# Three groups of M a batch, scores of batch 2 in fixed banks, and an earlier second weight block

## The chip, the cores and the metric

The kernel runs on one core of a Trainium2 chip. The metric is the time of one execution on the device in microseconds (us), as the median of three runs.

The core has five engines, each with its own in-order queue of instructions: TensorE (PE, matrix products), VectorE (DVE), ScalarE (ACT), GpSimd (POOL) and SyncE (SP, which here issues nearly all DMAs). They wait for one another through semaphores. PE writes to PSUM, which has eight banks of 128 partitions by 512 fp32 numbers. Everything else lives in SBUF or in HBM.

## The reference

Two blocks, one after the other. The first is an attention between 8 batches of 512 rows (8 heads of 64) and 32 states per head; the second is a two-layer network (FFN1, ELU, FFN2) over its output.

```python
scale = 1.0 / np.sqrt(D)                        # B, H, S, Ns, D = 8, 8, 512, 32, 64
a  = softmax(scale * x @ state.T)               # 512 x 32 per head
xread = a @ state
a2 = softmax(scale * state @ x.T)               # 32 x 512 per head
sread = a2 @ x
t = concatenate([xread, sread], axis=2)         # 544 rows per batch, 512 columns
h = t @ w_in                                    # 512 -> 2048
g = where(h > 0, h, exp(minimum(h, 0)) - 1)
out = g @ w_out                                 # 2048 -> 512
```

## The kernel before

**Folding the state into the weights.** `xread @ w_in` is `a @ (state @ w_in)`. So for each batch the kernel makes a matrix M = state @ w_in (256 rows, one for each head and state, by 2048 columns), and FFN1 is then a product of M with aT, the transposed attention weights. M is made from eight blocks of `w_in` of 256 columns each, called `hc` = 0 to 7. `make_m` (line 674) issues 8 matmuls per block on tiles of 64 rows by 32 columns of the array, four blocks of columns side by side. `copy_m` (692) takes the result from two banks to SBUF through ACT. Two neighbouring blocks form a chunk `c` of 512 columns, and FFN1 takes chunks 0 to 3 in turn.

**Fast products.** FFN1 and FFN2 of most batches use Strassen's scheme with seven products instead of eight, so sums of blocks of the operands are needed first: `sum_m` (707) and `sum_a` (716) make those of M and of aT on POOL, `Second.sums` and `combine` (965, 927) those of FFN2's operands on DVE. FFN2 of batches 1 to 7 nests the scheme: each of five outer products is a `Second` (941) with seven products of four matmuls 128x128, and the results are added from PSUM to the output by DVE (or copied by ACT). A product's bank, x or y, is written again by the next product but one.

**Phases.** `start` (1150) handles batches 0 and 1 together while the weights come in: x and state are loaded and transposed, scores and softmax run, blocks of `w_in` are converted to the number format that the products use (`convert`, 1090: two passes on ACT, four or five on DVE), each block is kept in a DRAM copy `w_in_mem`, and then `w_out` is converted too. `w_step(hc)` (1184) converts a block, makes its M for batches 0 and 1 and copies it out. FFN2 of batch 0 follows, then `ffn2_1` (1364) for batch 1, then `batch(b)` (1434) for b = 2 to 7, and `states` (1519) for the rows of `sread`.

**What batch b makes for b + 1.** In `ffn2` (1285) of batch b, `first_m` (1275) makes the M blocks 0 and 1 of batch b + 1, and `scores` makes its scores, in banks 6 and 7, which are called `fixed`. `soft_next` (1329) then runs the softmax in two forms: `softmax` for aT (subtraction of the maximum and the product with the reciprocal of the sum on POOL, transposes and maxima and sums on DVE, exponentials on ACT), and `softmax_rows` for `sread`. `move_state` (797) rearranges the latter with 16 small DMAs on SP, `state_read` (810) uses it. Later in `ffn2` blocks 2 and 3 of M are made; in `batch(b + 1)` 4 and 5, then 6 and 7. Each block comes from `w_in_mem` by `fetch` (669) into one of three slots, `w_half[:, hc % 3]`.

**What sets the order.** The code first records every operation in a `Plan` (87) with an estimated cost, and then a list scheduler (`run`, 239) decides in which order each engine's instructions are issued. PE takes the first operation in the order of recording that could start; DVE, ACT and SP take the one with the earliest due time, worked out backwards from PE's order; POOL keeps the recorded order strictly. A bank is given to an operation when it is free, except that the fixed ones wait for bank 6 or 7. The resulting queues are fixed in the program. In the first 40 us the scheduler also puts in filler matmuls on an identity (line 1590) where it expects PE to have nothing to do. `ident_ready` (1137) puts four matmuls of 128x128 into each fixed bank, before FFN2 of batch 1; nothing reads them.

Of the kernel before, what the change touches and what calls it, by code (L numbers as in the profile page):

```python
# [86 lines left out]
class Plan:  # L87
# [108 lines left out]
    def prepare(self):  # L196
        for op in self.ops:
            op.users = []
            op.turn = self.places.get(op.number, op.number)
        for op in self.ops:  # L200
            for d in op.deps:
                d.users.append(op)
        self.opening = {}
        self.closing = {}
        for b in self.banks:
            self.opening.setdefault(b.first, []).append(b)
            self.closing.setdefault(b.last, []).append(b)
        self.kept = {b.first: b.fixed for b in self.fixed}
        self.all_banks = min([op.number for op in self.kept], default=0)
# [29 lines left out]
    def run(self, until=0.0):  # L239
# [8 lines left out]
        banks = [(0.0, i) for i in range(self.BANKS)]  # L248
        fixed = set(self.kept.values())
        openers = sorted((op for op in self.ops if op in self.opening), key=lambda op: op.turn)  # L250
# [8 lines left out]
        def bank_time(op):  # L259

            if op in self.kept:
                return min([t for t, i in banks if i == self.kept[op]], default=None)
            need = len(self.opening[op])
            if op is not openers[oldest] and op.number > self.all_banks:
                need += self.KEPT_BANKS
            free = choice(op)
            return free[need - 1][0] if need <= len(free) else None
# [40 lines left out]
        while len(done) < len(self.ops):  # L308
# [26 lines left out]
            if op in self.kept:  # L335
                banks = [b for b in banks if b[1] != self.kept[op]]
                if self.kept[op] in holder:
                    after.append((holder[self.kept[op]], op))
            while oldest < len(openers) and openers[oldest] in opened:
# [50 lines left out]
def kernel(  # L390
# [165 lines left out]
    def bank():  # L556
        return Bank(plan).view()
# [116 lines left out]
    def make_m(b, *hcs):  # L674
# [11 lines left out]
        if hcs[-1] % 2 == 0:  # L686
            plan.ops[-1].spare = st[b, "m", c][0].bank

    def m_blocks(m):
        return [m[:, g * 512 + h * 256 : g * 512 + (h + 1) * 256] for h in range(2) for g in range(2)]  # L690
# [25 lines left out]
    def sum_a():  # L716

        r11, r12, r21, r22 = a_blocks_of(a_sb)
        t1, t2, t4 = (a_sb[:, 1024 + 256 * i : 1280 + 256 * i] for i in range(3))
        (V if 0 else Q).tensor_tensor(out=t1, in0=r12, in1=r11, op=ALU.subtract)  # L720
        (V if 0 else Q).tensor_tensor(out=t2, in0=r22, in1=t1, op=ALU.subtract)
        (V if 0 else Q).tensor_tensor(out=r12, in0=r22, in1=r12, op=ALU.subtract)
        (V if 0 else Q).tensor_tensor(out=t4, in0=r21, in1=t2, op=ALU.subtract)

# [35 lines left out]
    def softmax(b, to):  # L760
        s = st[b, "s"]
        total_t = small(b)[:, 36:68]

        def rows(g):
            return soft_t(b, g).rearrange("p (k n) -> p k n", n=NS)

        for g in range(G):
            V.transpose(out=soft_t(b, g), in_=s[g])
        for g in range(G):
            V.reduce_max(out=tops(b, g)["top_t"], in_=rows(g), axis=AX_X)  # L770
            (V if 0 & 1 and b > 1 or b in [] else Q).tensor_tensor(
                out=rows(g), in0=rows(g), in1=bc(tops(b, g)["top_t"], NS), op=ALU.subtract
            )
            A.activation(out=soft_t(b, g), in_=soft_t(b, g), func=AF.Exp, scale=scale)
            V.reduce_sum(out=tops(b, g)["total_t"], in_=rows(g), axis=AX_X)
        line(b, total_t, 1.0, eps)
        V.reciprocal(out=total_t, in_=total_t)
        for g in range(G):
            (V if 0 & 2 and b > 1 or b in [] else Q).tensor_tensor(
                out=rows(g), in0=rows(g), in1=bc(tops(b, g)["total_t"], NS), op=ALU.mult  # L780
            )
            V.transpose(out=to[:, g * 512 : (g + 1) * 512], in_=soft_t(b, g))
# [158 lines left out]
    class Second:  # L941
# [39 lines left out]
        def steps(self, out, fresh=False, base=None):  # L981

            t, s = self.t_w, self.s
            a11, a12, a22 = self.a
            x, y = bank(), bank()
            steps = []

            def step(n, ps, a, b, first, last, h, c):
# [9 lines left out]
                    "second",  # L998
                )
                o, p = (x[:, h, c * P : (c + 1) * P] for x in (out, base or out))  # L1000
                if n not in (0, 2, 3, 6):
                    p = o
                elif fresh:
                    p = None
# [6 lines left out]

            for n, args in enumerate((
                (x, a11, self.b11, True, False, 0, 0),
                (y, a12, self.b21, True, True, 0, 0),
                (x, s[2], t[2], False, False, 1, 0),
                (y, s[3], t[3], True, False, 1, 1),
                (x, s[1], t[1], False, False, 1, 1),
                (y, a22, t[4], False, True, 1, 0),
                (x, s[4], self.b22, False, True, 0, 1),
            )):  # L1020
                steps.append(lambda n=n, args=args: step(n, *args))
            return steps
# [127 lines left out]
    def start():  # L1150
# [21 lines left out]
        n = len(plan.ops)  # L1172
        load_states(0, 1, raw_s, (SP, ACT))
        load_x(0, x_halves, (SP, ACT))
        blocks[0] = weight_block(0, 2)
        load_states(1, 2, raw_s[:, 1:], (SP,))
        load_x(1, x_1)
        read_block(1)
        read_block(2)
        for k, op in enumerate(plan.ops[n:]):  # L1180
# [3 lines left out]
        def w_step(hc):  # L1184
            convert_block(hc)
            w = st["w", hc] = w_half[:, hc % 3]
# [14 lines left out]

        turn_x(x_halves, ob, 1)
        scores(0, ob)
        softmax(0, a_sb)
        w_step(0)
        ffn1(0, 0, (0, 1), 0 & 1)
        turn_x(x_1, ob)
        scores(1, ob)
        softmax(1, aT1)
        ffn1(1, 0, (0, 1), 0 & 2)  # L1210
        w_step(1)
        ffn1(0, 0, (2, 3))
        ffn1(1, 0, (2, 3))
        for c in range(1, 4):
            w_step(2 * c)
            w_step(2 * c + 1)
            ffn1(0, c)
            if c < 2:
                for b in range(2):
                    softmax_rows(b)  # L1220
                    turn_state(b)
                    state_read(b, (x_halves, x_1)[b])
            ffn1(1, c)
# [35 lines left out]
        o.copy(y, 1, 1)  # L1259
        scores(2, xr)  # L1260
        softmax(2, a_sb)
# [13 lines left out]
    def first_m(b, at=None):  # L1275
# [6 lines left out]
        fetch(2)  # L1282
        fetch(3)

    def ffn2(o, b):
# [3 lines left out]
        spare = spaces(m_sb[:, 1], 3)  # L1289
        o.sum_1()  # L1290
        late = [plan.ops[-1]]
        if 0:
            second[1].sums(o.a11, spare + s_2[0][:1])
            steps = second[1].steps(c12, fresh=True)
            steps[0]()
        else:
# [3 lines left out]
            steps = []  # L1300
        if nxt:
            first_m(b + 1, 1)
            scores(b + 1, xr, [f.view() for f in fixed])
        else:
            turn_read()
        for f in steps[1:]:
            f()
        second[2].sums(o.a12, s_2[1] + spaces(a_sb))
        late.append(plan.ops[-1])
        for f in second[2].steps(c11, base=c12):  # L1310
            f()
        late.append(plan.ops[-1])
        second[4].sums(o.a22, s_2[0] + spare[:2])
        late.append(plan.ops[-1])
        for f in second[4].steps(c21, fresh=True):
            f()
        second[6].sums(o.s, s_2[1] + spaces(a_sb))
        late.append(plan.ops[-1])
# [10 lines left out]
        def soft_next():  # L1329
            if nxt:  # L1330
                with plan.behind(late[4]):
                    softmax(b + 1, a_sb)
# [22 lines left out]
        if nxt:  # L1355
            make_m(b + 1, 2, 3)
            copy_m(b + 1, 1, m_to[1])
            sum_m(m_to[1])
            state_read(b + 1)
        for f in steps:  # L1360
# [3 lines left out]
    def ffn2_1(o, b, x1):  # L1364
# [30 lines left out]
        second[3].sums(o.a12, s_2[0])  # L1395
        make_m(b + 1, 2, 3)
        copy_m(b + 1, 1, m_to[1])
        sum_m(m_to[1])
        state_read(b + 1)
        for f in steps:  # L1400
# [33 lines left out]
    def batch(b):  # L1434
        for hc in range(4, 7):
            fetch(hc)
# [6 lines left out]
        p[0][0]()  # L1443
        p[1] = ffn1_chunk(b, 1, g_sb)
        p[0][1]()
        make_m(b, 4, 5)
        fetch(7)
        copy_m(b, 2, m_to[2])
        sum_m(m_to[2])
        p[1][0]()  # L1450
        p[2] = ffn1_chunk(b, 2, g_sb)
        p[1][1]()
        make_m(b, 6, 7)
        copy_m(b, 3, m_to[3])
        sum_m(m_to[3])
        if b + 1 < B:
# [122 lines left out]
    o, x1 = start()  # L1579
    ident_ready(0)  # L1580
    ident_ready(1)
    ffn2_1(o, 1, x1)
# [49 lines left out]
```

## Time and profile before

| | |
|---|---|
| median of three runs | 702.73 us (702.24 to 704.44) |
| the profiled execution | 704.65 us |
| its span, first to last instruction | 702.9 us |
| granted TensorE clock, mean | 0.997 |
| PE busy | 692.8 us (99%) |
| DVE busy | 563.8 us (80%) |
| ACT busy | 303.9 us (43%) |
| POOL busy | 144.2 us (21%) |
| DMA | 78.55 MB, mean 112 GB/s |

The span is that of the instructions; the profiled execution's own time is 1.75 us more. Busy shares are averages over the whole span, and the stages differ. These are the page's busy tenths in 40 equal slices of 17.6 us (9 is 90% or more):

```profile
PE   8899999999999999999999999999999999999997
DVE  4899999999649985899669985998589966997650
ACT  4899982011148122742176215712373227500530
POOL 1300000052211062303530181116220453000000
```

The first slices are the start with its loads; from the third on PE is full. DVE has nine tenths from 35 to 175 us, and ACT to 88 us, where weights are converted. From the twelfth slice on a pattern repeats about every 76 us, one batch: FFN1, with more work for ACT, and FFN2, with more for DVE.

Among the groups of instructions, POOL's are

```profile
L464 POOL TENSOR_TENSOR m<-m 128x256 f32<-128x256 f32 x72 | 63.6, 907 | 52.0 <-ACT m L464 50.6
L464 POOL TENSOR_TENSOR aT<-aT 128x256 f32<-128x256 f32 x24 | 22.3, 950 | 1.4 <-DVE aT L464 1.4
```

The columns are line, engine, operation, what it writes and reads, shapes and count, then the sum in us and the mean in ns, then the engine's idle time before. The first are the sums of M, the second those of aT.

### The profile page before, as it was taken

Reading aid. Unit: us, or ns where it says so; the run is one execution under the profiler, and the core shown is the slowest. Engines: PE = TensorE matmul, PEld = TensorE weight load, DVE = VectorE, ACT = ScalarE, POOL = GpSimd, SP = SyncE. Lnnn points to the kernel's source line nnn. Section 1 sums busy time; section 2 is a strip of 40 time slices with the busy share of each in tenths; the row PEclk is TensorE's granted clock in tenths of the full one; section 3 lists DMA queues with packets and bytes.
Section 4 is the critical chain, followed back from the end, with each engine's and each line's share of the span. In section 5 each row is a group of like instructions: output and inputs, shape, how many; then the busy total and the mean of one; then the engine's idle time right before and its main releaser. Section 6 shows DMA issues by size and latency. Waiting matters only on the chain.

```text
span 702.9 us, 14562 instructions
## 1 busy us (share of the span) xinstructions
PE 692.8 (99%) x5794; PEld 591.0 (84%) x5794; DVE 563.8 (80%) x991; ACT 303.9 (43%) x628; POOL 144.2 (21%) x161
## 2 busy tenths in 40 slices
PE   8899999999999999999999999999999999999997
PEld 7544468889988998889988998899888997899996
DVE  4899999999649985899669985998589966997650
ACT  4899982011148122742176215712373227500530
POOL 1300000052211062303530181116220453000000
PEclk9999999999999999999999999999999999999999
DMA  8578774204262505740471417450565034200300
GB/s 213 189 261 274 239 249 73 61 31 120 71 140 92 121 11 152 171 115 8 120 182 56 95 29 194 108 122 14 153 165 121 1 120 152 61 1 31 121 8 23
DMA packets 111268, 78.55 MB, mean 112 GB/s; under 512 B 89184, under 2 KB 92768, under 8 KB 111200
## 3 DMA queue, kind: packets, MB, share of 16 engines
q1 hardware_dynamic: 108988, 77.06, 39.4%
q8 instruction: 46, 0.75, 0.4%
q10 hardware_dynamic: 2212, 0.56, 0.4%
q14 instruction: 22, 0.18, 0.1%
HBM read 61.34 MB, written 13.11 MB: 106 GB/s over the span
## 4 chain that ended last, share of the span: by engine, by line
PE 94%; ACT 2%; DMA 2%; DVE 1%; SPq 1%; issue 0%; ACTq 0%; DVEq 0%
PE ps L464 93%; DMA g<-in_x_dram 1%; DMA xe<-in_x_dram 1%; SPq L464 1%; DVE w_half L464 1%; ACT sec L464 1%; ACT w_half L464 0%; ACT t_w L464 0%; PE ps L1590 0%; ACT m L464 0%; DVE sec L464 0%; DVE t_w L464 0%; ACTq L464 0%; DVE g L464 0%; ACT g L464 0%
## 5 line engine op out<-in xcount | busy, mean ns | idle before, releaser
L464 PE MATMUL ps<-aT,m 128*128 128x256 f32 (+1 forms) x568 | 149.7, 407 | 0.4 <-ACT m L464 0.4
L464 PE MATMUL ps<-w_out,g 128*128 128x128 f32 (+1 forms) x864 | 144.2, 315 | 0.0
L464 PEld LDWEIGHTS ps<-w_out,g 128*128 128x128 f32 x864 | 126.1, 191 | 14.9 <-issue 4.2
L464 PEld LDWEIGHTS ps<-aT,m 128*128 128x128 f32 x568 | 104.8, 190 | 33.3 <-issue 15.1
L464 DVE TENSOR_TENSOR o<-o,ps 128x128 f32<-128x128 f32 (+2 forms) x239 | 68.8, 289 | 66.9 <-PE ps L464 66.2
L464 ACT COPY o<-ps 128x128 f32<-128x128 f32 (+2 forms) x70 | 23.2, 335 | 158.7 <-PE ps L464 152.7
L464 POOL TENSOR_TENSOR xr<-xr,small 128x512 f32<-128x512 f32 x24 | 30.9, 1306 | 290.5 <-PE ps L464 147.1
L464 POOL TENSOR_TENSOR m<-m 128x256 f32<-128x256 f32 x72 | 63.6, 907 | 52.0 <-ACT m L464 50.6
L464 PE MATMUL ps<-sec 128*128 128x128 f32 x560 | 74.1, 275 | 0.0
L464 PEld LDWEIGHTS ps<-sec 128*128 128x128 f32 x560 | 68.5, 192 | 0.7 <-issue 0.4
L464 PE MATMUL ps<-t_w,s 128*128 128x128 f32 (+1 forms) x432 | 64.9, 298 | 0.0
L464 ACT ACTIVATE xe<-ps 128x512 f32<-128x512 f32 x96 | 54.4, 599 | 20.4 <-PE ps L464 15.0
L464 PEld LDWEIGHTS ps<-t_w,s 128*128 128x128 f32 x432 | 58.6, 192 | 3.3 <-ACT m L464 0.8
L464 ACT COPY m<-ps 128x512 f32<-128x512 f32 (+1 forms) x56 | 26.8, 535 | 55.6 <-PE ps L464 55.6
L464 DVE TENSOR_TENSOR ps<-sec,ps 128x512 f32<-128x512 f32 (+1 forms) x52 | 34.6, 673 | 17.5 <-PE ps L464 15.4
L464 DVE SCALAR_TENSOR_TENSOR g<-xe,ps 128x512 f32<-128x512 f32 x66 | 43.3, 684 | 1.7 <-ACT xe L464 1.1
L464 ACT COPY ps<-ps 128x512 f32<-128x512 f32 (+1 forms) x28 | 15.1, 541 | 61.2 <-PE ps L464 61.2
L464 ACT COPY sec<-ps 128x512 f32<-128x512 f32 (+1 forms) x52 | 29.7, 571 | 26.6 <-PE ps L464 18.5
L464 PE MATMUL ps<-aT,s 128*128 128x256 f32 x168 | 41.0, 379 | 0.0
L464 ACT ACTIVATE xe<-xe 128x512 f32<-128x512 f32 x66 | 38.8, 636 | 0.4
L464 PE MATMUL ps<-w_half,kT 64*32 64x256 f32 x1024 | 35.8, 382 | 0.6 <-DVE w_half L464 0.4
L464 PEld LDWEIGHTS ps<-aT,s 128*128 128x128 f32 x168 | 31.8, 190 | 4.5 <-DVE ps L464 0.2
(151 smaller groups left out, 1146.5 us busy)
## 6 DMA issues: line engine op xcount, KB each, us to landing
w_half<-w_in_mem SPq DMA_DIRECT2D x54, 512.0 KB
t_w<-in_moe_w_out_dram SPq DMA_DIRECT2D x8, 1024.0 KB
t_w<-in_moe_w_in_dram SPq DMA_DIRECT2D x7, 1024.0 KB
out_dram<-o SPq DMA_DIRECT2D x14, 512.0 KB
xe<-in_x_dram SPq DMA_DIRECT2D x26, 256.0 KB
o<-in_x_dram SPq DMA_DIRECT2D x80, 64.0 KB
w_in_mem<-w_half SPq DMA_DIRECT2D x8, 512.0 KB
xr<-xr SPq DMA_DIRECT2D x96, 32.0 KB
```

What stands on the lines that cost most here:

```text
L464: ins = getattr(engine, name)(**named)
```

## The change

It has several parts.

- M is made in three groups a batch: blocks 0 and 1, then 2, 3 and 4, then 5, 6 and 7. A group of three (`make_three`) takes four banks, two for the pair that forms a chunk and two for the single block, whose halves are copied by `copy_one`. `first_m` fetches one block more ahead, and `batch` the last three. The group of 2, 3 and 4 depends on a certain earlier product of `second`, so that it does not move ahead; `next_m` records it, and `state_read` after it.
- The scores of batch 2, in `start`, take the two fixed banks instead of any two. `kept` becomes a list, so that one operation may hold both. `ident_ready` is no longer called.
- In `start`, `w_step(1)` and the second half of FFN1 of chunk 0 of batch 0 are recorded ahead of the transposes, scores and softmax of batch 1.
- `sum_a` runs on DVE instead of POOL. So does the product with the reciprocal in the softmax of batches 0 and 1. Batch 0 takes the reciprocal for each half apart.
- `soft_next` follows `late[3]` (the sums of `second[6]`) instead of `late[4]` (the combination after it).

```diff
@@ Plan
-        self.kept = {b.first: b.fixed for b in self.fixed}
+        self.kept = {}
+        for b in self.fixed:
+            self.kept.setdefault(b.first, []).append(b.fixed)
@@ new functions
+    def make_three(b, pair, one):
+        c = pair[0] // 2
+        ps = st[b, "m", c] = [bank(), bank()]
+        half = st[b, "m", one] = [bank(), bank()]
+        calls = []
+        for hc in (*pair, one):
+            w, h = st["w", hc], hc % 2
+            calls.append(by_state(
+                b, half if hc == one else ps, [w[:, m] for m in range(NP)],
+                slice(0, 256) if hc == one else slice(h * 256, (h + 1) * 256), hc == one or h == 0,
+            ))
...
+            products(1.38, sum(calls, []), "make_m", "state")
+    def copy_one(b, hc, to):
+        for g in range(G):
+            A.copy(
+                out=to[:, g * 512 + hc % 2 * 256 :][:, :256], in_=st[b, "m", hc][g][:, :256],
+            )
+        g_of[b, hc // 2] = to
@@ sum_a (four times)
-        (V if 0 else Q).tensor_tensor(out=t1, in0=r12, in1=r11, op=ALU.subtract)
+        (V if 1 else Q).tensor_tensor(out=t1, in0=r12, in1=r11, op=ALU.subtract)
@@ softmax
-        line(b, total_t, 1.0, eps)
-        V.reciprocal(out=total_t, in_=total_t)
+        apart = b in [0]
+        if not apart:
+            line(b, total_t, 1.0, eps)
+            V.reciprocal(out=total_t, in_=total_t)
         for g in range(G):
-            (V if 0 & 2 and b > 1 or b in [] else Q).tensor_tensor(
+            if apart:
+                line(b, tops(b, g)["total_t"], 1.0, eps)
+                V.reciprocal(out=tops(b, g)["total_t"], in_=tops(b, g)["total_t"])
+            (V if 0 & 2 and b > 1 or b in [0, 1] else Q).tensor_tensor(
@@ start: x, s, w, f, X, S, F, 1, 2 name the steps of the old order
-        turn_x(x_halves, ob, 1)
-        scores(0, ob)
-        softmax(0, a_sb)
-        w_step(0)
-        ffn1(0, 0, (0, 1), 0 & 1)
-        turn_x(x_1, ob)
-        scores(1, ob)
-        softmax(1, aT1)
-        ffn1(1, 0, (0, 1), 0 & 2)
-        w_step(1)
-        ffn1(0, 0, (2, 3))
+        for what in 'xswf12XSF':
...
+            if what == "1": w_step(1)
+            if what == "2": ffn1(0, 0, (2, 3))
...
-        scores(2, xr)
+        scores(2, xr, [f.view() for f in fixed] if 1 else None)
@@ first_m
         fetch(3)
+        if 1: fetch(4)
+    def next_m(b):
...
+            before = [op for op in plan.ops if op.name == "second"][-7]
+            make_three(b, (2, 3), 4)
+            plan.ops[-1].deps.add(before)
...
+        copy_m(b, 1, m_to[1])
+        if 1: copy_one(b, 4, m_to[2])
+        sum_m(m_to[1])
+        if not 0:
+            state_read(b)
@@ ffn2
-                with plan.behind(late[4]):
+                with plan.behind(late[3]):
...
-            make_m(b + 1, 2, 3)
-            copy_m(b + 1, 1, m_to[1])
-            sum_m(m_to[1])
-            state_read(b + 1)
+            next_m(b + 1)
@@ batch
-        for hc in range(4, 7):
+        for hc in range(5, 8) if 1 else range(4, 7):
...
+        def m_three():
+            make_three(b, (6, 7), 5)
+            copy_one(b, 5, m_to[2])
+            copy_m(b, 3, m_to[3])
+            sum_m(m_to[2])
+            sum_m(m_to[3])
...
-        make_m(b, 4, 5)
-        fetch(7)
-        copy_m(b, 2, m_to[2])
-        sum_m(m_to[2])
+        if mm == 3: m_three()
         p[1][0]()
...
-        make_m(b, 6, 7)
-        copy_m(b, 3, m_to[3])
-        sum_m(m_to[3])
@@ the end
-    ident_ready(0)
-    ident_ready(1)
+    if not 1:
+        ident_ready(0)
+        ident_ready(1)
```

## The prediction

> **What bounds the kernel now.** I read three views in this order: the chain of waits, the engines' busy time by stage, and TensorE's timeline. The chain that ended last is TensorE almost throughout:
>
> ```profile
> PE 94%; ACT 2%; DMA 2%; DVE 1%; SPq 1%; issue 0%; ACTq 0%; DVEq 0%
> ```
>
> By stage (from:to and length in us, then busy us of PE, PEld, DVE, ACT, POOL with instruction counts, granted clock, DMA share, GB/s):
>
> ```profile
> 20.00:21.00 1.00, 1.00 (x7) 0.99 (x5) 1.00 (x2) 1.00 (x3) 1.00 (x2) 0.50 1.01 389
> ...
> 48.00:97.00 49.00, 49.00 (x323) 22.09 (x322) 45.63 (x60) 46.74 (x86) 0.00 (x0) 1.00 0.76 254
> 161.00:197.80 36.80, 36.80 (x423) 34.98 (x423) 27.48 (x59) 4.75 (x12) 7.71 (x8) 1.00 0.32 100
> ```
>
> From 48 us on PE has no gap until the tail at 698. There, only what leaves PE's own stream counts; DVE (27.5 of 36.8 us in the second stage), ACT and POOL are covered unless they become late. Before 48 us, PE still waits on loads, ACT and DVE, and for some 3 us runs at half clock. The timeline of PE (start, us, engine, line, operation, out<-in, tiles, count; each fp32 matmul of the program is two instructions):
>
> ```profile
> 38.98 7.03 PE L464 MATMUL ps<-s,g 128*128 128x512 f32 x16
> 45.94 1.09 PE L464 MATMUL ps<-w_half,kT 64*32 64x256 f32 x32
> ...
> 47.83 1.49 PE L464 MATMUL ps<-w_half,kT 64*32 64x256 f32 x32 [0.21 <-ACT m L464]
> 49.25 7.13 PE L464 MATMUL ps<-aT,m 128*128 128x512 f32 x16
> ...
> 81.23 1.53 PE L464 MATMUL ps<-w_half,kT 64*32 64x256 f32 x48
> 82.68 7.13 PE L464 MATMUL ps<-aT,m 128*128 128x512 f32 x16
> ...
> 160.61 1.95 PE L464 MATMUL ps<-w_out 128*128 128x128 f32 x16
> 162.39 1.95 PE L464 MATMUL ps<-t_w,s 128*128 128x128 f32 x16
> ...
> 197.76 1.89 PE L464 MATMUL ps<-aT,m 128*128 128x256 f32 x8
> 199.59 1.09 PE L464 MATMUL ps<-w_half,kT 64*32 64x256 f32 x32
> 200.61 8.90 PE L464 MATMUL ps<-aT,m 128*128 128x256 f32 x40
> 209.44 1.09 PE L464 MATMUL ps<-w_half,kT 64*32 64x256 f32 x32
> ```
>
> Rows overlap at their ends, so I take times from start to start. The rows `ps<-w_half,kT` are the making of M, the only 64x32-tile work between full-array matmuls.
>
> **Step 1: `ident_ready` goes.** It is the row at 160.61, 8 matmuls whose result nobody reads: 162.39 - 160.61 = **1.78 us** of PE. Nothing waits behind it that needs the time: the sums for the row at 162.39 are ready, and in the new order DVE reaches them earlier, since batch 2's softmax (12 instructions of about 0.6 us) now stands behind them.
>
> **Step 2: three M groups a batch.** The matmuls stay the same; a group less is opened and closed. A full-array run of 128x256 goes at 0.216 us an instruction (8 take 1.73 us at 214.02 to 215.75). The 8 before the group at 199.59 took 1.83 (+0.10), the 40 after it 8.83 instead of 8.65 (+0.18, of which 0.10 is the next entry): **0.18** around a group. Inside, 32 instructions take 1.02 (200.61 - 199.59) and 48 take 1.45 (82.68 - 81.23): 0.43 for each 16, so 0.16 is fixed. One group: 0.34 us; batches 2 to 7 each lose one: 6 x 0.34 = **2.04 us**. Bounds: 1.1 (only what lies around the group) to 2.2 us.
> The new group of three takes four banks instead of two, and `make_three` is made to follow a given `second` product. PE is in order, so all later products queue behind it; they wait if its block of w_in or its banks are late. The banks come free through ACT copies, two of 0.40 and two of 0.59 us, against six full-array products of 0.86 us beside them; ACT has 4.75 busy of 36.8 us. The block comes by SP: the batch's fetches 5, 6 and 7 now stand directly behind the 16 DMAs of `move_state`. Batch 4's moves were issued over 10.1 us, ending 8.7 us after its second M group started. Three fetches of 512 KB at about 300 GB/s (from 271 to 276.3 us the DMAs moved 1.6 MB) need 5.2 us more plus 1.5 us of issue: 15.4 us after that start. By the new order the third group comes 17.1 us after it (1.45 for the group itself, 12 `second` products of 0.89, 3.5 of FFN1, 1.03 of `state_read`, 0.4 for entries). Hidden, with 1.7 us to spare. The next batch's fetches 0 and 1, which wait for that group, now precede all 16 `load_blocks`; these have from 200 to the scores at 232.33, against 14 us of issue and landing. Hidden too.
>
> **Step 3: scores(2) into the fixed banks.** They must find both banks empty, and move on PE from 138.76 to behind the two products at 162.39: 22 us later, same cost. What they issue moves along: the softmax (12 DVE, 4 POOL, 7 ACT instructions), 4 `load_x` and 16 `move_state` DMAs on SP. The chain from scores to the last aT sum took 139.85 to 158.2 = 18.4 us, that to the last move's issue 139.85 to 169.8 = 30 us, a store and a fetch among them. The new one starts near 162.4: sums by 181, moves by 188 to 192. First users: the second product of FFN1 of batch 2 near 195, and `state_read` near 193. I take 0; if cover fails, up to 2.7 us.
>
> **Step 4: sums of aT, and the softmax products of batches 0 and 1, on DVE.** POOL loses 24 sums of 0.95 us, DVE gains 24 of about 0.34 (half of a 128x512 sum's 0.6 pitch, and the overhead); the four products are part of step 5. That batch b+1's softmax may follow `late[3]` lets it start one pair of sums earlier, under a full PE: 0. In batches 3 to 7 they lie where PE is full and DVE is not: 0. At batch 2, DVE has most to do: I count about 23 us of sums and softmax and 6 us of 128x128 adds in the 36 us from 160. Here a rule weighs against the row. DVE's columns as above, then POOL's:
>
> ```profile
> 168.05 1.01 DVE L464 TENSOR_TENSOR sec<-t_w,sec 128x512 f32<-128x512 f32 x1
> ...
> 174.35 0.69 DVE L464 TENSOR_TENSOR sec<-sec,s 128x512 f32<-128x512 f32 x1
> ```
> ```profile
> 166.65 4.12 POOL L464 TENSOR_TENSOR m<-m 128x256 f32<-128x256 f32 x4 [8.46 <-ACT m L464]
> ```
>
> A DVE sum beside POOL's took 1.01 instead of 0.69: +0.32. The Trainium skill, "SBUF — State Buffer", section "SBUF: two separate sides", says that a DVE instruction with two SBUF inputs and a GpSimd instruction hold the shared port alone, and the other fully blocks. POOL's 13 us here (4 softmax at 1.3, 8 M sums at 1.0) would then come whole on top of 29: 42 us in 36, a stall of 6 us. By the row it is 12 x 0.32 = 4 us: 33 in 36, no stall. I take the row.
>
> **Step 5: the second block ahead of batch 1's softmax.** Only this needs the in-order queues followed, with durations from the rows of 18 to 50 us. DVE finishes block 0 near 20.5 instead of 25.1, since the port is free of POOL's products; M of block 1 starts near 29 instead of 33.51. (The loads of blocks 3 and 4 and the store of block 1 are issued earlier with it; blocks 1 and 2 have landed by 22 us, when the DMA share falls to 0.20.) But batch 1's aT stands behind it: ACT reaches its last row exponential near 36, six filler matmuls (1.9 us) stand before FFN1 of batch 1, which I put at 38.8 against 38.98. By then the second half of `turn_state` (0.66 us) is done that before came at 46.97, and `state_read` (1.03) goes before FFN1 of chunk 1 of batch 0, at 49.4 against 49.25. Net **0.9 us**, estimated; bounds -0.5 (loss) to 2.5.
> The rule that speaks against more: the clock is 0.50 in the row at 20 us, and PE stood 1.7 us in pieces between 15 and 18.7. The Trainium skill, "TensorE: Matmul & The Clock Gate", section "What's actually happening", lets activity in a window of 3.4 us set the clock. The change leaves those gaps (x of batch 1 lands at 18.65 either way) and takes one 0.66 us transpose out of them. By the rule about 3.2 us run at half clock again; were the row a chance of this execution, about 1.5 us more would be gained. I take the rule.
>
> **The sum.** 1.78 + 2.04 + 0.9 = **4.7 us**. The profiled execution took 704.65 us with a span of 702.9; it should come to 699.9 and 698.2. It lies 1.9 us above the median of the runs, 702.73, for which I forecast **698.0**.
>
> **Rivals.**
> - *The start gives back* (or batch 2 stalls): ACT's queue holds more ahead of batch 1's softmax, or step 3 loses its cover. For it: ACT and DVE are full from 18 to 36 us. Against it: M of block 1 comes 4 us earlier. Start 0 and a stall up to 2.7: 698.9 to 701.6, say 700.3.
> - *The clock stays full* near 20 us: 698.0 - 1.5 = 696.5. For it: the rest of the span is at 1.00. Against it: the same gaps.
> - *The change doesn't save a group*: the third group waits for its fetches and the 2.04 are lost: 700.0. For it: only 1.7 us to spare.
> - *Slower: the aT sums show on PE.* In each `second` block a product may overwrite its bank only after DVE has read it, one product (0.89 us) later; a sum queued between two adds delays that. All 24 on PE cost 24 x 0.34 = 8.2 us: 702.73 - 4.7 + 8.2 = 706.2; slower once more than 4.7 of the 8.2 land. Against it: near the end of `second` DVE idles 0.6 us before each add at 188 to 198, and 1.1 and 1.8 us at 272 and 274.
>
> **Chances.** Forecast 0.62 (own range 696.8 to 699.5), start gives back 0.15, clock 0.14, no group saved 0.04, slower 0.05. The range 695.4 to 701.3 holds the first four for the most part. A measurement tells 0.3% (2.1 us) from no change: below 700.6 lie the forecast, the clock, the lost group and half of the first rival: faster 0.87; same 0.08; slower 0.05.
>
> **What would show it.** Right: no `ps<-w_out` row of 16; M rows of 32, 48 and 48 per batch, a period of batches 0.3 us shorter; PE without gaps after 50 us; six aT sums' places on DVE at about 0.35 us. Wrong: PE waiting on a `w_half` load at the third group, on `aT` near 195, or DVE named before `second` products. If the period of batches falls by 0.1 us or rises, step 2 is wrong.

## The result and the profile after

The changed kernel takes **698.45 us** (median of four runs, 697.83 to 699.04); the kernel before took 702.62 us beside it (702.24 to 704.44). The ratio is 0.9935, with an interval of 0.9915 to 0.9955. The forecast was 698.0 us, in a range from 695.4 to 701.3.

Here is the same view of the stages as before (from:to and length in us, busy us of PE, PEld, DVE, ACT, POOL, granted clock, DMA share, GB/s), then the chain that ended last:

```profile
20.00:21.00 1.00, 0.67 (x16) 0.38 (x24) 1.00 (x4) 0.97 (x4) 0.00 (x0) 1.00 1.02 377
...
48.00:97.00 49.00, 48.73 (x248) 22.48 (x247) 46.36 (x60) 46.83 (x83) 0.00 (x0) 1.00 0.76 248
161.00:197.80 36.80, 36.33 (x457) 33.18 (x456) 29.38 (x67) 8.72 (x25) 11.97 (x12) 1.00 0.38 117
```
```profile
PE 89%; ACT 4%; DMA 3%; DVE 2%; issue 1%; POOL 0%; SPq 0%; ACTq 0%; POOLq 0%
PE ps L466 88%; DMA w_half<-w_in_mem 3%; ACT sec L466 2%; DVE sec L466 1%; PE ps L1706 1%; DVE w_half L466 1%; ACT w_half L466 1%; ACT t_w L466 1%; ACT o L466 0%; ACT g L466 0%; ACT m L466 0%; DVE t_w L466 0%; ACT xr L466 0%; DVE s L466 0%; DVE o L466 0%
```

The first row has the clock at 1.00 where it was 0.50. In the last two stages PE is short of full by 0.27 and 0.47 us; before it was full. And a transfer that the chain of before didn't name stands there with 3%: `w_half<-w_in_mem`, the fetched block of `w_in`. (The chain counts whole transfers; PE itself stood still for 0.8 us in two waits for it.) PE's timeline shows both sides of step 2:

```profile
156.76 1.95 PE L466 MATMUL ps<-t_w,s 128*128 128x128 f32 x16
158.64 1.09 PE L466 MATMUL ps<-xr,kT 64*32 64x512 f32 x16
...
175.37 1.53 PE L466 MATMUL ps<-w_half,kT 64*32 64x256 f32 x48
...
195.16 0.66 PE L466 MATMUL ps<-w_half,kT 64*32 64x256 f32 x16
196.29 1.10 PE L466 MATMUL ps<-w_half,kT 64*32 64x256 f32 x32 [0.47 <-DMA w_half<-w_in_mem]
...
499.43 1.10 PE L466 MATMUL ps<-w_half,kT 64*32 64x256 f32 x32 [0.34 <-DMA w_half<-w_in_mem]
```

The filler row is gone, the scores of batch 2 stand behind the row that followed it, and the second group has 48 instructions in one piece. The third group (from 195.16) stops after block 6 and waits for block 7.

Where the time went, by the starts of the same work in both traces. The profiled execution of before had one stretch of 3.413 us at half clock. Two later runs with the same start and full clock reach the scores of batch 2 at 137.15 and 137.19 us instead of 138.76, so I take 1.6 us off all later times of before (its span would be 701.3):

| | before, less 1.6 | after | difference |
|---|---|---|---|
| first product of `w_out` | 94.92 | 93.89 | -1.0 |
| FFN1 of batch 2 starts | 196.16 | 193.34 | -2.8 |
| M of blocks 0, 1 for batch 3 | 229.84 | 226.87 | -3.0 |
| M of blocks 0, 1 for batch 7 | 533.02 | 528.29 | -4.7 |
| span | 701.3 | 696.3 | -5.0 |

### The profile page after: what moved, and what is told of

Its sections match the earlier page's. It is cut to its first block, busy times and chain, and to the rows that moved or that the text cites. A ratio compares the mean times of both kernels' runs of the same rounds, so it can differ in the third digit from the quotient of the medians.

```text
span 696.3 us, 14561 instructions
## 1 busy us (share of the span) xinstructions
PE 686.0 (99%) x5778; PEld 590.8 (85%) x5778; DVE 571.3 (82%) x1020; ACT 302.9 (44%) x641; POOL 112.6 (16%) x133
## 4 chain that ended last, share of the span: by engine, by line
PE 89%; ACT 4%; DMA 3%; DVE 2%; issue 1%; POOL 0%; SPq 0%; ACTq 0%; POOLq 0%
PE ps L466 88%; DMA w_half<-w_in_mem 3%; ACT sec L466 2%; DVE sec L466 1%; PE ps L1706 1%; DVE w_half L466 1%; ACT w_half L466 1%; ACT t_w L466 1%; ACT o L466 0%; ACT g L466 0%; ACT m L466 0%; DVE t_w L466 0%; ACT xr L466 0%; DVE s L466 0%; DVE o L466 0%
## 5 line engine op out<-in xcount | busy, mean ns | idle before, releaser
L466 PE MATMUL ps<-aT,m 128*128 128x256 f32 (+1 forms) x568 | 147.9, 405 | 0.1
L466 PEld LDWEIGHTS ps<-aT,m 128*128 128x128 f32 x568 | 106.2, 190 | 29.1 <-issue 14.5
L466 DVE TENSOR_TENSOR o<-o,ps 128x128 f32<-128x128 f32 (+2 forms) x239 | 67.2, 285 | 41.5 <-PE ps L466 40.7
L466 POOL TENSOR_TENSOR m<-m 128x256 f32<-128x256 f32 x72 | 60.4, 859 | 27.2 <-ACT m L466 25.8
```

Source lines behind the costliest of these rows:

```text
L466: ins = getattr(engine, name)(**named)
```

## The experiments

Each is one edit. The times of before in their four sets of runs were 703.16, 703.12, 703.22 and 703.18 us. One thing to know for all: an edit gives the list scheduler another problem, and it may lay out stretches anew that the edit doesn't name. So I compared the order of PE's instructions too, and say where it moved.

### The filler, and the scores in the fixed banks

The kernel before without `ident_ready`:

```diff
-    ident_ready(0)
-    ident_ready(1)
```

> The kernel before without the two calls of ident_ready, nothing else changed. The forecast's step 1: eight matmuls leave a PE that has no gap, so 1.78 us less, 700.8 us, ratio 0.9975; PE's row of 16 at 160.6 us is gone and the row after it follows at once. Rival: those 1.78 us cover sums on DVE that are late (in the trace of before a product near 169.3 us takes 1.13 instead of 0.89 us); then some of it comes back as waits of PE for DVE behind that place: 701 to 702.6 us. Leaves out matmuls that nobody reads; no part of the computation.

Measured: 700.91 us, ratio 0.9967 (0.9959 to 0.9974). This kernel doesn't compute the same. By the code the place is FFN1 of batch 2: in `ffn1_chunk` ACT copies a partial sum into a fixed bank, and the next products are to add to it. From batch 3 on, scores have stood in these banks before; for batch 2, `ident_ready` is there. So the prediction's "matmuls whose result nobody reads" missed their purpose: not the values are needed, but that TensorE has written the banks. The Trainium skill, "PSUM — Partial Sum Buffer", section "The four PSUM rules", has the reason: a matmul that doesn't open an accumulation adds only where an earlier matmul has marked the place as written, and ACT's writes don't mark. No trace shows marks; what the runs show is that the result differs without the matmuls, and doesn't with the scores of batch 2 in their place. So steps 1 and 3 are one. Next, these two alone:

```diff
-        scores(2, xr)
+        scores(2, xr, [f.view() for f in fixed])
...
-    ident_ready(0)
-    ident_ready(1)
```

> The kernel before, with batch 2's scores put into the two fixed banks behind the product that ends the second FFN2, and without ident_ready: steps 1 and 3 of the prediction together, nothing else. If the scores' new place costs nothing: 1.8 us less than before by the row, up to 2.3 by the run without the filler alone, so 700.9 to 701.3. If step 3's cover fails (batch 2's weights or moves come late): up to 2.7 us of it back, 702 to 704, with a wait on aT or a DMA near 195 us.

Measured: 700.48 us, ratio 0.996 (0.9947 to 0.9973): 2.6 us less than before, a little more than expected. By its trace the making of M for batch 3 starts at 227.74 us, against 229.84: 2.1 us, 1.8 of it the filler's row. No wait on aT or on a move appears near 195. The new place costs nothing.

### The sums of aT on DVE

```diff
-        (V if 0 else Q).tensor_tensor(out=t1, in0=r12, in1=r11, op=ALU.subtract)
+        (V if 1 else Q).tensor_tensor(out=t1, in0=r12, in1=r11, op=ALU.subtract)
```

and likewise for the other three sums, on the kernel before (V is DVE, Q is POOL).

> The kernel before with aT's sums on DVE instead of POOL, nothing else. Forecast's step 4: no change, within 0.5 us of 702.6. Its rival: 24 sums of 0.34 us delay additions that PE's products wait for, up to 8.2 us more, 710.8 us; any PE wait for DVE in the second products would show it. The shared port: DVE's other sums beside POOL get shorter where POOL's aT sums are gone.

Measured: 701.56 us, ratio 0.998 (0.9973 to 0.9986). Neither expectation: it is 1.6 us **faster**. Batches follow each other after 75.53 to 75.58 us instead of 75.80. FFN1 shows where, first before, then this kernel (start, us, what PE does):

```profile
279.70 4.71 PE L464 MATMUL ps<-aT,m 128*128 128x256 f32 x20
284.24 1.03 PE L464 MATMUL ps<-aT,s 128*128 128x256 f32 x4
```
```profile
276.68 6.31 PE L466 MATMUL ps<-aT,m 128*128 128x256 f32 x28
282.92 1.09 PE L466 MATMUL ps<-w_half,kT 64*32 64x256 f32 x32
```

At 0.216 us each, with 0.10 to enter from the M group, 20 instructions need 4.42 us and took 4.54; 28 with 0.10 to enter and 0.09 to leave need 6.24 and took 6.24. Before had 0.12 us of small waits there and 0.10 more near 301, in every batch from 3 on; both are gone. That is 0.22 x 5 = 1.1 of the 1.6 us; the rest had come by batch 3's M, which starts at 229.29 us instead of 229.84. But the scheduler has also laid FFN1 out anew, as the rows show (28 instructions in one run, where before turned to the products `aT,s` after 20). So the edit as a whole is worth 1.6 us, and which part of it took the waits away is not shown: POOL's work on the shared port, its lateness, or the new order. What DVE paid for a sum stands in the groups of the changed kernel (count, busy us, mean ns):

```profile
L466 DVE TENSOR_TENSOR aT<-aT 128x256 f32<-128x256 f32 x24 | 9.6, 421 | 0.0
```

It is 421 ns against POOL's 950 (forecast: 340), and hidden.

### The order of the start

The kernel before with the second block ahead of batch 1's softmax, the softmax products of batches 0 and 1 on DVE, and batch 0's reciprocal for each half apart:

```diff
-        for what in 'xswfXSF12':
+        for what in 'xswf12XSF':
...
-            (V if 0 & 2 and b > 1 or b in [] else Q).tensor_tensor(
+            (V if 0 & 2 and b > 1 or b in [0, 1] else Q).tensor_tensor(
```

> The kernel before with the start's new order and the softmax products of batches 0 and 1 on DVE; all else as before. Forecast's step 5: 0.9 us less by the order of the queues, 701.8 us. Rival: the trace of the change reached the first product of w_out 2.6 us earlier than the trace of before, and if all of that belongs to the new order the runs come out at 700.1 us. Second rival: the 3.4 us at half clock in the trace of before are a matter of that one execution, come in some executions of each kernel, and make 1.6 us of those 2.6; then the runs show 1 us, and this kernel's own profile shows the half clock or not by chance.

Measured: 701.79 us, ratio 0.998 (0.9973 to 0.9987): 1.4 us less. The scores of batch 2 start at 136.07 us instead of 137.15, so 1.1 us is the start's own; the rest has come by batch 3's M (1.5 us earlier), in a stretch of batch 2 that was laid out anew. Now the order alone undone in the change (the softmax products stay on DVE):

```diff
-        for what in 'xswf12XSF':
+        for what in 'xswfXSF12':
```

> The change, with the second block of w_in converted behind batch 1's softmax again, as before. Theory: with groups of three the planner lays the old start into finer pieces, with TensorE waiting for ACT's copies of M, as it did where the groups were tried alone; the first product of w_out begins near 98 us instead of 93.9: 702 to 702.6. Rival: the start is worth what it is worth by itself (1.1 to 1.4 us), independent of the groups: 699.6, first product of w_out near 95.

Measured: **709.36 us**, ratio 1.0081 (1.0062 to 1.01), slower than before and 11 us slower than the change; both expectations are far off. Its timeline and stages:

```profile
52.53 1.38 PE L466 MATMUL ps<-w_half,kT 64*32 64x256 f32 x16 [2.77 <-ACT m L466]
53.84 3.04 PE L466 MATMUL ps<-aT,m 128*128 128x512 f32 x4
...
83.32 7.13 PE L466 MATMUL ps<-s,g 128*128 128x512 f32 x16 [1.76 <-DVE sec L466]
...
108.65 0.59 PE L466 MATMUL ps<-sec,xr 64*128 64x64 f32 x12
```
```profile
18.00:25.00 7.00, 6.16 (x72) 3.61 (x70) 6.11 (x13) 4.62 (x12) 0.00 (x0) 0.53 1.01 318
...
48.00:56.00 8.00, 5.10 (x36) 1.83 (x36) 4.85 (x8) 5.61 (x13) 0.00 (x0) 0.79 0.98 359
```

With groups of three and the old order, the scheduler cuts the start into pieces: FFN1 runs in fours between single blocks of M, and PE waits for ACT's copies of M (4.5 us in all) and for DVE. The row at 108.65 stands at 95.71 in the change. In this execution the clock was halved for 10.2 us as well (about 18.4 to 25.2, and 52.5 to 56): up to 5 of these 13 us. But one execution of this kernel had a mean clock of 1.0, and it took 707.57 us: some 9 of the 11 us are there without half clock. The second stretch of half clock begins where the wait of 2.77 us ends, and four instructions at 53.84 take 3.04 us, against 1.98 at full clock.

### The groups of three

On the kernel before, the groups of three together with two more parts of the change, the aT sums on DVE and the softmax behind `late[3]`. The groups without these two were not measured.

```diff
+        if 1: fetch(4)
...
-            make_m(b, 2, 3)
+            make_three(b, (2, 3), 4)
...
-        make_m(b, 4, 5)
...
-        make_m(b, 6, 7)
+            make_three(b, (6, 7), 5)
```

> The kernel before with the three groups of M alone, and with the two parts that the schedule of the groups can't do without: aT's sums on DVE and the softmax behind late[3]. The start, the scores of batch 2 and ident_ready are as before. Forecast's step 2: 2.04 us less, 700.6 us. What the trace of the change suggests: 0.37 us for each of six groups and some 0.2 us of small waits in FFN1 of five batches, less three waits of 0.3 to 0.5 us for the last block: 2 us less all the same, with periods of batches of 75.2 us instead of 75.8 where no wait falls. Rival (the aT sums show on PE): 6 to 8 us more.

Measured: 703.1 us, ratio 0.9999 (0.9991 to 1.0007). No gain, as if the groups were worth nothing. But the first product of `w_out` starts at 98.10 us, 3.2 later than with the aT sums alone (94.94): the same broken start, in a milder form (the softmax products of batches 0 and 1 are on POOL here). Behind it batches take 75.22 to 75.53 us. The converse, pairs again in the change, keeps its start instruction for instruction:

```diff
-            make_three(b, (2, 3), 4)
+            make_m(b, 2, 3)
...
-        mm = 3
+        mm = 0
```

> The change, with M of blocks 2 to 7 made in three pairs again (four groups a batch). Its start on TensorE is that of the change, instruction for instruction, which the earlier run with the groups alone lacked. If a group is worth 0.35 us a batch and the waits for block 7 give 1.2 us of it back: 698.4 + 6 x 0.35 - 1.2 = 699.3; period of batches 75.55 us instead of 75.21. If the groups are worth nothing, as the run with them alone had it: 698.4. By the prediction's step 2 (2.04, all hidden): 700.4.

Measured: 701.24 us, ratio 0.997 (0.996 to 0.9981), with 698.5 for the change in the same runs: the groups are worth 2.7 us there. Its batches take 75.64 to 76.22 us, on the mean worse than the four-group kernels with the order of before (75.80, and 75.56 with the sums on DVE). So 2.7 is the price of a group plus what that new order loses. The group itself is better read from the aT sums alone (75.56, four groups) and the batches of the change without a wait (75.21, three): 75.56 - 75.21 = **0.35 us** a batch. The two orders differ in more than the group, but the prediction's sum from single rows, 0.34, agrees.

### The change itself, twice more

> The change itself, beside the three other kernels of this call, so that they can be compared on one chip: 698.4 us, ratio 0.993 to 0.994 to the kernel before. If half clock near 20 us belongs to every execution of a kernel whose start has these gaps (the rule of the prediction), its profile shows a row of 0.50 there; if it is a chance of one execution, most profiles show none.

> The change itself, beside the two others of this call: 698.4 us.

Measured: 698.5 us, ratio 0.993 (0.9916 to 0.9944), and 698.24 us, 0.9929 (0.9911 to 0.9946). No profile has a half clock near 20 us. But the third group pauses in all of them, each time in other places. By how much later the next work starts, it is 0.7, 0.6 and 0.3 us in batches 2, 6 and 7 in the first profile, 1.2 in batch 6 in the second, 1.2 in batch 2 and 0.55 in batch 6 in the third. That is 1.2 to 1.8 us in an execution.

Not all of it is block 7. In the first profile and in batch 2 of the third, PE stops at a block's border and the trace names `w_half`. In batch 6 of the second and third it stops after 36 of 48 instructions, where the borders are at 16 and 32, and no transfer is named ("issue": nothing that the profile shows). The second profile:

```profile
497.75 1.49 PE L466 MATMUL ps<-w_half,kT 64*32 64x256 f32 x36
499.79 0.65 PE L466 MATMUL ps<-w_half,kT 64*32 64x256 f32 x12 [0.55 <-issue]
```

### Can the pauses of the third group be removed?

Three ways. First, block 5 ahead of 6 and 7 in the third group:

```diff
-        for hc in (*pair, one):
+        for hc in ((one, *pair) if one == 5 else (*pair, one)):
```

> The change, with the third group's matmuls in the order 5, 6, 7 instead of 6, 7, 5. The third group waited for block 7 in three of six batches, by 0.47, 0.34 and 0.40 us, with the 0.43 us of block 5 still to do behind the wait. If only the last of the three blocks is late, block 5's matmuls cover these waits: less than 0.1 us is left of each, and the time is 1.1 us under the change's, 697.3. If the blocks land together, or the wait comes with block 5 or 6, nothing changes: 698.4.

Measured: 699.55 us (697.03 to 700.63), ratio 0.994 (0.9922 to 0.9958): not told apart from the change. In the profile batch 6 still waits:

```profile
497.75 2.06 PE L466 MATMUL ps<-w_half,kT 64*32 64x256 f32 x48
499.74 3.50 PE L466 MATMUL ps<-aT,m 128*128 128x256 f32 x15
```

1.99 us from start to start instead of 1.45. By PE's weight loads it stops after 37 of 48 here, with no transfer named: nearly the same place in PE's queue, though the blocks come in another order. So this pause doesn't hang on block 7, and the profile holds no wait for `w_half` that the new order could have covered. One thing fits: a 16 KB transfer that the trace calls "instruction" starts 0.8 us before the group here, and 0.4 and 0.9 us before it where the pause was 1.2 and 0.55 us. Ahead of it the DMA engines are full (share 0.98 from 493 to 497 us in the second profile). That PE waits for it is not shown. Second, the fetches on ACT's queue, so that SP's 16 moves are not ahead of them:

```diff
-            fetch(hc)
+            fetch(hc, queue=ACT)
```

> The change, with the batch's fetches of blocks 5, 6 and 7 issued by ACT, right behind the copies of the second group of M, instead of by SP behind the 16 moves. Theory: in the change these fetches land at about the moment the third group needs them; it waits 0.5 to 1.2 us in some batches of some executions (1.4 us in all in the first profile of the change, 1.2 in the second), and this is also the spread of its times (697.0 to 700.6 with the order of blocks changed). Issued some 8 us earlier they are in place: no wait for w_half in the profile, all batches 75.2 us apart, and 697.2 us with a spread under 1 us. Rival: the spread has another cause, or the fetches only push the moves or stores back by as much: 698.4 again, with the wait on another transfer.

Measured: **702.81 us**, ratio 0.9996 (0.9984 to 1.0008); the whole gain is gone. No wait for `w_half` is left, but ACT and then PE show this (ACTq is ACT issuing DMAs):

```profile
256.76 1.07 ACT L466 COPY m<-ps 128x512 f32<-128x512 f32 x2 [1.71 <-PE ps L466]
257.40 6.07 ACTq L466 DMA_DIRECT2D w_half<-w_in_mem  x3
263.50 0.65 ACT L466 COPY s<-ps 128x256 f32<-128x256 f32 x2 [5.67 <-DMA xr<-xr]
```
```profile
263.93 1.99 PE L466 MATMUL ps<-aT,m 128*128 128x256 f32 x8 [0.38 <-ACT s L466]
```

The three issues took 6.07 us in place of 1.5 to 2.9 on SP, until a move of SP (`xr<-xr`) had landed. Behind them in ACT's order stood two copies of M, and PE's next FFN1 product waited for these. In other batches ACT stood 5.5 and 5.8 us before these copies, at 415 and 491 us. From 260 us on, PE waits four times for such a copy, 1.6 us together, and batches follow each other after 75.79 to 76.27 us instead of 75.21. Third, the fetches stay on SP, but are due 12 us earlier in the plan:

```diff
-            fetch(hc)
+            fetch(hc)
+            plan.ops[-1].nudge = 12
```

> The change, with the fetches of blocks 5, 6 and 7 kept on SP, but due 12 us earlier in the planner: from batch 3 on they stand behind the first 5 to 7 of the 16 moves instead of behind all; in batch 2 they can't come earlier. Theory: the third group's waits for w_half after batch 2 go (0.0 to 1.2 us in the three profiles of the change, 0.7 on the mean), and the moves that come 2 us later show nowhere, since the planner puts state_read behind FFN1's first matmuls: 697.6 us. Rival: as with the fetches on ACT, what is put ahead of the moves comes back as a wait elsewhere (moves, stores or state_read late): 699 us or more.

Measured: **697.26 us** (696.76 to 698.0), ratio 0.9918 (0.9907 to 0.993). SP's queue in batch 6 and what PE then does:

```profile
478.36 4.73 SPq L466 DMA_DIRECT2D xr<-xr  x7
483.19 1.48 SPq L466 DMA_DIRECT2D w_half<-w_in_mem  x3
484.72 7.24 SPq L466 DMA_DIRECT2D xr<-xr  x9
```
```profile
498.17 1.53 PE L466 MATMUL ps<-w_half,kT 64*32 64x256 f32 x48
499.63 3.72 PE L466 MATMUL ps<-aT,m 128*128 128x256 f32 x16
```

The fetches leave 7 us earlier, at 483 instead of 490 to 491, and the group runs through in 1.46 us. The "instruction" transfer, too, now starts at 495.0, 3.1 us before the group, so which of the two took the pause away isn't told apart. In batch 2, where they can't come earlier, 0.40 us of waiting is left, and batch 4 takes 75.55 us for a reason that was not looked for. This kernel is the fastest of all, about 1 us under the change; since its interval overlaps the change's, and 0.56 us of the difference of the two profiles lies in the start, where both have the same order on PE, only the vanished pause of batch 6 is shown, not the full microsecond.

## Why the prediction was right, and which terms were off

The time was right to 0.5 us, and the sum too: 4.7 us against 5.0 from a before at full clock to after. Two terms were wrong and made up for each other, so the closeness is in part luck.

- **Step 1** (1.78): right in size. The row's 1.78 us left PE and nothing took its place. Wrong was that nobody needs the matmuls; step 3 is what permits leaving them out.
- **Step 2** (2.04, "hidden, with 1.7 us to spare"): the price of a group was right (0.34 predicted, 0.35 measured, 2.1 us for six). The cover was not: pauses of the third group give 1.2 to 1.8 us back, most of it (1.6 in the first profile) as waits for block 7. The term that failed most is the landing of the fetches, 1.5 us of issue and 5.2 more for 1.6 MB. In the first profile block 7's products start 9.1 us after the issue begins in batch 2 (187.17 to 196.29) and 8.5 us after it in batch 6 (490.98 to 499.43), not 6.7. In these stretches the DMAs moved 2.4 and 2.5 MB (263 and 293 GB/s): two stores of 512 KB go out beside the three fetches, and they were left out of the sum. The moves were late as well: the fetches' issue began 11.8 us after the second group in batch 2 and 9.6 in batch 6, not 8.7. In batch 2 most of that was taken up, as the third group came 19.8 us after the second and not 17.1; in batch 6 it came after 17.05. That rival ("no group saved", 0.04) was nearer than I held it to be.
- **Step 3** (0): right; the pair with step 1 gained at least step 1's price.
- **Step 4** (0): mis-sized. Alone it gained 1.6 us, 1.1 of it as 0.22 us a batch, since with the new order small waits in FFN1 went that I had not looked for: I called PE full from 48 us on, and at the resolution of busy shares it was. On the rule that was weighed (a full block on the shared port, 6 us of stall at batch 2) the row was the better guide: no stall appeared.
- **Step 5** (0.9): 1.0 to 1.1 us in the start, right in size. The rule behind it, that gaps bring the half clock back each time, was wrong as I used it: three kernels with the start of before, and three profiles of the change with its gaps, ran at 1.00. It was a chance of the execution, though not a rare one: of 109 executions of before beside the experiments, 18 had a mean clock of 0.997 or less, as the profiled one had, with a median span of 702.6 us against 701.2 of the others. Of the change's 15, 2 had it. (Where in them the clock was lower is not on record.) It did no harm to the forecast, since the saving was carried over to the medians, and these are at full clock on both sides: before's span without the 1.6 us, and the 1.75 us around it, make 703.05, against medians of 702.6 to 703.2. For the same reason the rival in which the clock stays full had its mechanism right and its 1.5 us wrong.
- **The slower rival** (aT sums show on PE, 706.2) was refuted, with the opposite sign.

What I had not seen at all is how the parts hang together: taken alone, the groups gain nothing and the start 1.4 us; with the groups in and the old start back, 11 us are lost. The parts' gains alone sum to 2.6 + 1.6 + 1.4 = 5.6 us and the groups' 2.1 don't appear there; in the whole, the account is 1.8 (filler) + 0.6 (groups less waits) + 1.1 (aT sums) + 1.0 (start) = 4.5 of 5.0 us. Of the 0.5 left, 0.24 can be seen: a product of before at 168.18 us held PE for 1.13 instead of 0.89 us, and the stretch, laid out anew, has no such wait in the change. The rest is not assigned.

## What to carry to other kernels

Where a scheduler lays out the queues, an edit taken alone measures the layout as well as the edit: check which stretches moved, and read the price of a thing from periods without stalls. A prefetch is as early as the last instruction ahead of it in its queue; move it up among small DMAs of the same queue before giving it to an engine that has copies to make. A "useless" matmul may be there for the state that it leaves in a bank.

## What the runs showed of the hardware

- With the same matmuls on 64x32 tiles, one group less between full-array products saved TensorE 0.35 us.
- Half clock came in one stretch of 3.413 us in a profile of before, in none of eleven profiles of other kernels with that start or the change's (a mean clock of 0.997 or less in 18 of 109 executions of before, 2 of 15 of the change), and in stretches of 6.827 and 3.413 us in the one kernel whose start has PE waits of up to 2.77 us.
- The issue of three DMAs of 512 KB took ACT up to 6.07 us while SP's 16 small moves were under way, against 1.5 to 2.9 us for the same three on SP behind the moves. Whether the queue or the program's semaphores held them, these runs don't tell.
- PE paused 0.5 to 1.2 us inside a row of like matmuls in three profiles, at nearly the same place in its queue and with no releaser in the trace, when a 16 KB transfer of the kind "instruction" had started less than 1 us before the row; where it had started 3.1 us before, there was no pause. Whether it is the cause is open.
